# A pre-norm transformer block: the output's copy, the maxima's transposition and the number of maxima in a group are placed anew

## The chip, the cores and the metric

The kernel runs on one core of one Trainium2 chip. The metric is device time in microseconds (us) for one execution. Where a profile is quoted, the engines are PE (TensorE, matrix products), PEld (its weight loads), DVE (VectorE), ACT (ScalarE), POOL (GpSimd) and SP (SyncE, which issues all DMAs here). L75 is line 75 of the kernel; most instructions are recorded by small helpers (`mm` L75, `tr` L78, `pool` L82, `act` L89, `dve` L92, `dma` L95), so tiles' names tell more than lines do.

## What is computed

One sequence of S = 2048 rows, D = 512 columns, in float32. The reference, cut to what matters:

```python
h  = x + attention(layernorm(x), wqkv) @ wo      # 32 heads of 16 columns
h2 = h + silu(layernorm(h) @ w1) @ w2            # 1792 columns in between

scores = einsum("bhqd,bhkd->bhqk", q, k) * 16 ** -0.5
o      = einsum("bhqk,bhkd->bhqd", softmax(scores), v)
```

The softmax runs over all 2048 keys.

## The kernel before, in words

**Numbers.** A value is held as a high part and a low part. In projections and MLP a product is three matrix products (high x high, low x high, high x low) in `product` (L109). The high part is a copy by ScalarE, the low part a subtraction by `low` (L97) on VectorE or GpSimd.

**Items and groups.** The attention is cut into 32 *items*, each of four heads and 512 query rows; eight items make a block of 512 rows. An item has 16 *groups*, one for each 128 keys, so there are 512 groups; `g` counts them, and `i, c = divmod(g, 16)` are the item and the place in it. In a group there are four `scores` (L474; a product of 64 rows of the array, an exponential by ScalarE into `pt`), and the four heads' `values` (L485) of two groups earlier, which add into one PSUM bank `pv`. When the last group of an item has been added (in the group c = 1 of the next item), `finish_item` (L500) copies `pv` to `pvs` and sends it off by five DMAs; sums of the exponentials come back by DMA some groups later, are inverted by VectorE (`rc`), spread by DMA (`den`), and multiplied in by GpSimd.

**Maxima.** The exponentials need each row's maximum of scores beforehand. So each item has 64 *maxima* (`maximum`, L206): a product of 48 rows into a bank `ps_m`, and a reduction over 512 columns by VectorE into `mx`. There are 2048 of them. When an item's 64 are done, `finish_max` (L219) reduces them to `nm`, GpSimd splits these in two half-precision parts, and two steps later (`WAIT`) `place_max` (L234) transposes them on TensorE (`ps_n`), copies them to `mt` and sends them by DMA into the item's queries, where the product of `scores` then adds them in. Heads lie on the upper or the lower 64 rows of the array (*halves*); a score and a maximum on different halves can run side by side. `one_max` (L266) takes the next maximum of the item in hand, on the half that is asked for, or on the other if that half has none left.

**Where the maxima go.** They are spread over the whole program: `burst` puts some beside the projections of queries, keys and values (the first 200 us), the planner `maxima(g)` (L821) says how many come in each group of the attention, and `mlp` (L637) weaves bursts into its products. The planner takes a rate from what must be done by which item, less what the MLP blocks will take (`BESIDE`), and allows three in a group, or four beside the output projection of blocks 1 to 3. In the attention, the m-th score of a group is followed by a maximum on the other half, for as many m as there are maxima.

**Blocks.** After the items 8, 16 and 24 (`FIRSTS`) a block's output projection is done in groups c = 10 to 15 of that item (`output`, L676), and two groups into the next item the MLP of the block runs by itself (`finish_block`, `mlp`): 14 steps f, each a product of 12 matrix products with w1, `gate` (L613: SiLU, high and low part), and 12 matrix products with w2 of the step before (`second`). A dictionary such as `{4: 3, 12: 3}, {8: 4}` says: three maxima after the fourth product with w1, three after the twelfth, and four after the eighth with w2. `BESIDE_C[1]` is used for the steps in `EXTRA`, `QUIET` is the step from which there are none. The last block's MLP (`finish_last`) comes at the end.

**Queues and banks.** Each engine works in the order in which the program names its instructions, and waits in that order. PSUM in the attention: one bank for `pv`, three for maxima (`sm`), four for scores and the rest (`st`). In the projections of `wqk` that follow the first four units there are two `st` and six `sm`. `place_max` uses `sm` in the attention and `st` before it. In the MLP the bank `pv` takes the products with w1, and the first of four maxima.

Of the kernel before, what the change touches and what calls it, by code (L numbers as in the profile page):

```python
# [12 lines left out]
F16 = mybir.dt.float16  # L13
# [7 lines left out]
P = 128  # L21
# [6 lines left out]
FC = F // P  # L28
NB = S // 512
# [18 lines left out]

FIRSTS = 8, 16, 24

WAIT = 2
AHEAD = 4


BESIDE = (132, 132, 106)
OUTPUT = 9

BESIDE_A = {6: 6}, {4: 4}

BESIDE_C = ({4: 3, 12: 3}, {8: 4}), ({4: 3, 10: 3}, {4: 3, 10: 4})  # L60

EXTRA = (), (), ()

QUIET = FC, FC, FC - 2


@with_exitstack
def attention_mlp_kernel(ctx: ExitStack, tc: tile.TileContext, x, wqkv, wo, w1, w2, out):
# [19 lines left out]
    def act(fn, *a, **k):  # L88
        pin(getattr(nc.scalar, fn)(*a, **k))  # L89
# [38 lines left out]
    def bank(name, kind="st", dtype=F32):  # L128
        return banks[kind].tile([P, 512], dtype, tag=kind, name=name)
# [103 lines left out]

    def place_max(i, ns):  # L234

        ps = bank("ps_n", "sm" if at["attention"] else "st", F16)
        tr(ps[:32, :P], ns.rearrange("p j r a -> p (j r a)"), ident_h)
        mt = small.tile([32, P], F16, name="mt")
        act("copy", mt, ps[:32, :P])
        for j in range(2):  # L240
            dst = qs[i % RING][64 * j + 48:64 * j + 50].rearrange("r a n -> r (a n)")
            pin(nc.sync.dma_start(dst.rearrange("r (a b) -> r a b", b=P), mt[16 * j:16 * j + 16, :]))
        placed.add(i)
# [2 lines left out]
    todo = {(i, j): [(i, kb, qt, a, j) for kb in range(4) for a in range(2) for qt in range(4)]  # L246
            for i in range(ITEMS) for j in range(2)}
    END = 64 * ITEMS
    at = {"item": 0, "done": 0, "half": 0, "step": 0, "due": 0, "attention": False}
    agenda = {}  # L250

    def soon(steps, fn, *a):
# [8 lines left out]
    def next_item():  # L261
        while at["item"] < ITEMS and not (todo[at["item"], 0] or todo[at["item"], 1]):
            at["item"] += 1
        return at["item"]

    def one_max(half=None, ps=None):  # L266

        i = next_item()
        if i == ITEMS:
            return  # L270
        if half is None:
            half = at["half"]
            at["half"] = 1 - half
        half = half if todo[i, half] else 1 - half
        at["done"] += 1
        if maximum(*todo[i, half].pop(0), ps):
            soon(WAIT, place_max, i, finish_max(i))

    def burst(n, *more):
        for ps in more:  # L280
# [11 lines left out]
    with ExitStack() as pa:  # L292
# [114 lines left out]
        for b in range(NB):  # L407
            units = [("qk", 1), ("qk", 0)]
            vs = [("v", t) for t in range(4)]
            found = {}  # L410
            for n, (kind, k) in enumerate(vs + units if b == 0 else units + vs):
                tick()
                if b == 0 and n == 3:
                    measure()
                if kind == "v":
                    project_v(b, k)
                else:
                    project_qk(b, k)
                    if k == 0:
                        for i in range(2):  # L420
                            for h in range(4):
                                if b == 0:
                                    load_q(i, h)
                                load_k(i, h, b * 512, 512)
                if b == NB - 1:
                    burst(5)
                elif b > 0 and n > 1:
                    burst(4)
                if b + 1 < NB:
                    rows = xts[b + 1]  # L430
# [12 lines left out]
        pool("memset", va[:, :, :, DH:DH + 1], 1.0)  # L443

        pb.close()
        open_banks(pa, 1, st=2, sm=6)
        for g in range(1, NG // 2):
            for m, (b, key) in enumerate([(b, 1) for b in range(NB)] + [(b, 0) for b in range(NB)]):
# [51 lines left out]
    def finish_item(i):  # L500
# [3 lines left out]
        if i == ITEMS - 1:  # L504
            act("copy", pvs[:, :256], pv[:, :256])
            dve("tensor_copy", pvs[:, 256:], pv[:, 256:])
        else:
            act("copy", pvs, pv)
        if i == ITEMS - 1:
            last.append(pvs)  # L510
            return
# [98 lines left out]
    def turn_rows(t):  # L610
        turn(hx.pop(t), hth[:, :, t * P:(t + 1) * P], htl[:, :, t * P:(t + 1) * P])

    def gate(ps):  # L613
        g, gh, gl = (bp.tile([P, 512], dt, tag="pt", name=name)
                     for name, dt in (("g", F32), ("gh", F32R), ("gl", F32R)))
        act("activation", g, ps, AF.Silu)
        act("copy", gh, g)
        low(gl, g, gh)
        return gh, gl

    def second(b, acc, f, gh, gl, inserts={}):
# [15 lines left out]
    def mlp(b):  # L637
# [10 lines left out]
        for f in range(FC):  # L648
# [11 lines left out]
            for kind, n in (("w2", f), ("w1", f + 1)) if f else (("w1", 1), ("w2", 0)):  # L660
# [1 line left out]
            ps = pv if f else first  # L662
            weave(product(ps, lambda c: w1h[:, c, :], lambda c: w1l[:, c, :],
                          lambda c: hth[:, c, :], lambda c: htl[:, c, :], DC), beside_1)
            parts = gate(ps)
            if f == FC - 1:

                act("activation", small.tile([P, 1], F32, name="sw"), ident[:, :1], AF.Exp)
# [152 lines left out]
    def maxima(g):  # L821
# [12 lines left out]
        if g in marks or g - 1 in marks:  # L834

            return 0
        most = 4 if i in FIRSTS and OUTPUT < c < OUTPUT + 5 else 3
        n = max(0, min(most, int(at["due"]), ready - at["done"]))
        at["due"] -= n
        return n  # L840
# [3 lines left out]
    for g in range(groups):  # L844
        tick()
        i, c = divmod(g, KC)
        if g in marks:
            finish_block(i // 8 - 1, (g - 2, g - 1))
        if i + RING - 1 < ITEMS and 6 <= c < 14:
# [23 lines left out]
                    soon(5, split_weights, "w1", f, "dve", "dve")  # L873
        if g == 1:
            dve("memset", pv, 0.0)
        n = maxima(g)
        for m in range(4):
            k = m ^ (g % 2)
# [42 lines left out]
```

## Time and profile before

| | |
|---|---|
| median of 3 runs | 1712.84 us (1711.66 to 1714.91) |
| the profiled execution | 1715.59 us |
| its span, first to last instruction | 1713.8 us |
| mean granted TensorE clock | 0.998 |
| reductions `mx<-ps_m` on DVE | 2013 in 1261.5 us busy |
| exponentials `pt<-ps_s` on ACT | 2048 in 1017.8 us busy |
| copies `pvs<-pv` on ACT | 32 in 20.5 us busy |

The profile is one execution on the chip. Busy times are sums over an engine's instructions; matrix products are pipelined, so their durations overlap and a busy TensorE is not one at its peak. The *chain of waits* follows the last instruction back: at each step to what released it, or to the instruction before it on its engine. Its lines give the start, the length, the engine, the tile written and the number of instructions. A *window* is a stretch of the span with each engine's busy time in it. In groups of instructions, the numbers behind the bar are the busy time in us, the mean duration in ns, and the engine's idle time before them with what ended it.

### The profile page before, as it was taken

Reading aid. Unit: us, or ns where it says so; the run is one execution under the profiler, and the core shown is the slowest. Engines: PE = TensorE matmul, PEld = TensorE weight load, DVE = VectorE, ACT = ScalarE, POOL = GpSimd, SP = SyncE. Lnnn points to the kernel's source line nnn. Section 1 sums busy time; section 2 is a strip of 40 time slices with the busy share of each in tenths; the row PEclk is TensorE's granted clock in tenths of the full one; section 3 lists DMA queues with packets and bytes.
Section 4 is the critical chain, followed back from the end, with each engine's and each line's share of the span. In section 5 each row is a group of like instructions: output and inputs, shape, how many; then the busy total and the mean of one; then the engine's idle time right before and its main releaser. Section 6 shows DMA issues by size and latency. Waiting matters only on the chain.

```text
span 1713.8 us, 28253 instructions
## 1 busy us (share of the span) xinstructions
PE 1672.5 (98%) x10498; PEld 647.6 (38%) x10498; DVE 1449.2 (85%) x2399; ACT 1254.9 (73%) x2494; POOL 233.2 (14%) x318
## 2 busy tenths in 40 slices
PE   7999999999999999999989999999999999999999
PEld 5656422222245542222235542222235542221377
DVE  6899999999978889999978889999978869997243
ACT  4323599999963369999963369999963379999743
POOL 2113300000033310000033310000023310000000
PEclk9999999999999999999999999999999999999999
DMA  6334411111222211111222211111212211100222
GB/s 186 99 85 139 123 33 44 36 44 43 59 60 79 68 49 31 36 46 41 60 58 81 62 53 32 36 41 46 57 56 84 64 46 39 35 11 20 57 80 80
DMA packets 100570, 102.81 MB, mean 60 GB/s; under 512 B 19028, under 2 KB 77204, under 8 KB 100432
## 3 DMA queue, kind: packets, MB, share of 16 engines
q1 hardware_dynamic: 100432, 101.01, 20.2%
q8 instruction: 82, 1.34, 0.3%
q14 instruction: 56, 0.46, 0.1%
HBM read 77.72 MB, written 17.29 MB: 55 GB/s over the span
## 4 chain that ended last, share of the span: by engine, by line
PE 56%; ACT 37%; DVE 4%; issue 2%; DMA 1%; POOL 0%; SPq 0%; ACTq 0%; POOLq 0%; DVEq 0%
ACT pt L89 36%; PE pv L75 18%; PE ps_acc L75 10%; PE ps_s L75 8%; PE ps_m L75 7%; PE ps_qk L75 5%; PE ps_v L75 3%; PE ps_w L75 3%; DVE mx L215 2%; PE ps_wo L75 2%; PE ps_tr L78 1%; ACT pvs L89 1%; DVE ot L92 0%; DVE st L92 0%; DVE gl L92 0%
## 5 line engine op out<-in xcount | busy, mean ns | idle before, releaser
L215 DVE TENSOR_REDUCE mx<-ps_m 128x1 f32<-128x512 f32 x2013 | 1261.5, 684 | 104.7 <-PE ps_m L75 74.2
L89 ACT ACTIVATE pt<-ps_s 128x512 f32<-128x512 f32 x2048 | 1017.8, 662 | 16.2 <-PE ps_m L75 9.6
L75 PE MATMUL ps_s<-qs,ks 64*128 64x512 f16 x2048 | 546.2, 380 | 8.0 <-ACT pt L89 2.4
L75 PE MATMUL pv<-pt,va 128*17 128x512 f32 x4096 | 538.3, 599 | 1.3
L75 PE MATMUL ps_m<-ks,qs 48*128 48x512 f16 x2013 | 516.7, 381 | 7.7 <-DVE mx L215 6.9
L75 PEld LDWEIGHTS <-ks 64*128 64x128 f16 x2048 | 152.6, 95 | 547.0 <-issue 438.3
L75 PEld LDWEIGHTS pv<-pt,va 128*17 128x17 f32 x4096 | 68.8, 95 | 234.5 <-issue 219.5
L75 PEld LDWEIGHTS <-qs 48*128 48x128 f16 x2048 | 120.2, 94 | 69.6 <-issue 65.4
L89 ACT CAST w2h<-w 128x512 fp32r<-128x512 f32 x56 | 34.8, 621 | 90.8 <-PE ps_acc L75 90.8
L89 ACT ACTIVATE g<-pv 128x512 f32<-128x512 f32 x39 | 23.3, 598 | 103.8 <-PE pv L75 103.8
L82 POOL TENSOR_SCALAR nm<-nm 128x16 f32<-128x16 f32 x32 | 8.5, 265 | 663.3 <-DVE nm L222 663.3
L75 PE MATMUL ps_acc<-w2l,gh 128*128 128x512 f32 x224 | 92.6, 413 | 0.0
L75 PE MATMUL ps_acc<-w2h,gh 128*128 128x512 f32 x224 | 92.2, 412 | 0.0
L75 PE MATMUL ps_acc<-w2h,gl 128*128 128x512 f32 x224 | 88.2, 394 | 0.0
L92 DVE TENSOR_TENSOR gl<-g,gh 128x512 fp32r<-128x512 f32 x56 | 41.2, 736 | 53.3 <-ACT gh L89 53.3
L82 POOL TENSOR_TENSOR w2l<-w,w2h 128x512 fp32r<-128x512 f32 x42 | 53.5, 1274 | 182.3 <-ACT w2h L89 182.3
L75 PE MATMUL pv<-hth,w1l 128*128 128x512 f32 x156 | 65.5, 420 | 0.0
L82 POOL TENSOR_TENSOR ot<-ot,den 128x512 f32<-128x512 f32 (+1 forms) x16 | 20.4, 1274 | 317.6 <-DMA den<-dr 286.6
L89 ACT ACTIVATE ks<-ps_qk,qk_s 128x512 f32<-128x512 f32 x24 | 16.6, 690 | 62.5 <-PE ps_qk L75 62.5
L75 PE MATMUL pv<-hth,w1h 128*128 128x512 f32 x156 | 62.1, 398 | 0.0
L75 PE MATMUL pv<-htl,w1h 128*128 128x512 f32 x156 | 61.4, 394 | 0.0
L82 POOL TENSOR_TENSOR w1l<-w,w1h 128x512 fp32r<-128x512 f32 x42 | 55.6, 1324 | 15.5 <-ACT w1h L89 15.5
(119 smaller groups left out, 1315.9 us busy)
## 6 DMA issues: line engine op xcount, KB each, us to landing
w<-in_B_w_dram SPq DMA_DIRECT2D x112, 256.0 KB
ks<-kd SPq DMA_DIRECT2D x120, 192.0 KB
qs<-qd SPq DMA_DIRECT2D x128, 48.0 KB
kd<-sh SPq DMA_DIRECT2D x16, 256.0 KB
qd<-sh SPq DMA_DIRECT2D x16, 256.0 KB
hx<-in_A_x_dram SPq DMA_DIRECT2D x16, 256.0 KB
out_dram<-ot SPq DMA_DIRECT2D x16, 256.0 KB
ot<-pvs SPq DMA_DIRECT2D x124, 32.0 KB
```

Source lines behind the costliest of these rows:

```text
L75: tc.keep_in_program_order(nc.tensor.matmul(*a, **k))
L78: tc.keep_in_program_order(nc.tensor.transpose(*a))
L82: tc.keep_in_program_order(getattr(nc.gpsimd, op)(*a, **k))
L89: pin(getattr(nc.scalar, fn)(*a, **k))
L92: pin(getattr(nc.vector, fn)(*a, **k))
L215: pin(nc.vector.tensor_reduce(mx[i][:, j, a, qt, kb:kb + 1], ps, axis=AX.X, op=ALU.max))
```

## The change

- `finish_item`: `pv` is copied by VectorE, except for the items 8, 16, 24 (ScalarE as before) and the last one.
- `place_max`: always takes a bank `sm`; in the attention VectorE copies to `mt`.
- `due_at` (new): a transposition that falls due in the attention is put off to the next group with c = 2 (`JOINT`), which follows the group that ends with the output's copy, unless that is too near the item's own scores or in an item after 8, 16 or 24. In a group c = 2 the planner allows two maxima.
- `one_max`: where the half asked for has none left, it takes the next item's, if that item's operands are loaded and the item in hand is more than 12 groups away; in the first projections it takes from items 0 and 1, whichever has the earlier keys.
- Planner: at most three maxima in all other groups, also beside the output projection.
- MLP: steps 4, 7 and 10 of the first two blocks have 13 maxima; the first burst comes after the fifth product; the last block has maxima up to step 12; `gate` of the first step subtracts on GpSimd.
- First projections: six maxima beside the last block's queries and keys (five before); from the second block on, the scaled product goes to SBUF and its low part `sl` is made by GpSimd.

```diff
+JOINT = 2
-BESIDE = (132, 132, 106)
+BESIDE = (141, 141, 122)
+BESIDE_V = (0, 4), (0, 4), (6, 5)
-BESIDE_C = ({4: 3, 12: 3}, {8: 4}), ({4: 3, 10: 3}, {4: 3, 10: 4})
+BESIDE_C = ({5: 3, 12: 3}, {8: 4}), ({4: 3, 10: 3}, {4: 3, 10: 4})
-EXTRA = (), (), ()
+EXTRA = (4, 7, 10), (4, 7, 10), ()
-QUIET = FC, FC, FC - 2
+QUIET = FC, FC, FC - 1
...
     def place_max(i, ns):
-        ps = bank("ps_n", "sm" if at["attention"] else "st", F16)
+        ps = bank("ps_n", "sm", F16)
...
-        act("copy", mt, ps[:32, :P])
+        if at["attention"]:
+            dve("tensor_copy", mt, ps[:32, :P])
+        else:
+            act("copy", mt, ps[:32, :P])
...
+    def due_at(i):
+        g = at["group"]
+        if g is None:
+            return WAIT
+        joint = g + WAIT + (JOINT - g - WAIT) % KC
+        return joint - g if joint < KC * i - 2 and joint // KC - 1 not in (-1, *FIRSTS) else WAIT
...
     def one_max(half=None, ps=None):
...
+        if at["blocks"]:
+            i = min(range(2), key=lambda n: (todo[n, half] or todo[n, 1 - half] or [(n, KC)])[0][1])
+        elif not todo[i, half] and 64 * (i + 2) <= at["ready"] and KC * i - at["next"] > 12:
+            i += 1
...
-            soon(WAIT, place_max, i, finish_max(i))
+            soon(due_at(i), place_max, i, finish_max(i))
...
-                    project_qk(b, k)
+                    project_qk(b, k, scale=b > 0)
...
-                if b == NB - 1:
-                    burst(5)
-                elif b > 0 and n > 1:
-                    burst(4)
+                if b:
+                    burst(BESIDE_V[b - 1][kind == "v"])
...
     def finish_item(i):
...
-        else:
-            act("copy", pvs, pv)
+        elif i in FIRSTS:
+            act("copy", pvs, pv)
+        else:
+            dve("tensor_copy", pvs, pv)
...
-    def gate(ps):
+    def gate(ps, engine="dve"):
...
-        low(gl, g, gh)
+        low(gl, g, gh, engine)
...
-            parts = gate(ps)
+            parts = gate(ps, "dve" if f else "pool")
...
     def maxima(g):
...
-        most = 4 if i in FIRSTS and OUTPUT < c < OUTPUT + 5 else 3
+        at["ready"] = ready
+        most = 2 if c == JOINT and i and i - 1 not in FIRSTS else 3
```

More of the change, by code (lines that the diff above doesn't have):

```diff
@@ L248, in attention_mlp_kernel @@
     END = 64 * ITEMS
-    at = {"item": 0, "done": 0, "half": 0, "step": 0, "due": 0, "attention": False}
+    at = {"item": 0, "done": 0, "half": 0, "step": 0, "due": 0, "attention": False, "group": None, "ready": 0, "next": 0, "blocks": True}
     agenda = {}
@@ L445, in attention_mlp_kernel @@
         pb.close()
+        at["blocks"] = False
         open_banks(pa, 1, st=2, sm=6)
@@ L846, in attention_mlp_kernel @@
         i, c = divmod(g, KC)
+        at["group"], at["next"] = None, g
         if g in marks:
@@ L875, in attention_mlp_kernel @@
             dve("memset", pv, 0.0)
+        at["group"] = g
         n = maxima(g)
```

## The prediction

> **What bounds the kernel now.** I read the page's busy shares and chain first, then the chain of waits inside the attention, then windows of the other stages.
>
> ```profile
> PE 1672.5 (98%) x10498; PEld 647.6 (38%) x10498; DVE 1449.2 (85%) x2399; ACT 1254.9 (73%) x2494; POOL 233.2 (14%) x318
> PE 56%; ACT 37%; DVE 4%; issue 2%; DMA 1%; POOL 0%; SPq 0%; ACTq 0%; POOLq 0%; DVEq 0%
> ```
>
> TensorE hardly rests, and the chain changes between it and ScalarE. Now the chain in one item of the attention, in which `ps_s` are scores, `ps_m` maxima and `pv` the value products:
>
> ```profile
> 302.84 0.48 ACT pvs L89
> ...
> 305.72 0.98 PE pv L75 x8
> 306.70 0.32 PE ps_s L75
> 307.02 0.22 PE ps_m L75 x2
> ...
> 307.68 0.98 PE pv L75 x8
> ...
> 335.46 29.45 ACT pt L89 x60
> ```
>
> A group lasts 1.96 us (305.72 to 307.68): 0.98 of values and 0.98 of four score slots, in which the three maxima run beside scores on the other half of the array's rows. ScalarE's four exponentials come to the same: 29.45 / 60 x 4 = 1.96. So 16 groups are 31.4 us, and two things come on top in each item. The first is the output's copy, read from TensorE's timeline:
>
> ```profile
> 301.30 1.05 PE L75 MATMUL pv<-pt,va 128*17 128x512 f32 x8
> ...
> 303.37 1.05 PE L75 MATMUL pv<-pt,va 128*17 128x512 f32 x8
> ...
> 305.65 0.62 PE L75 MATMUL pv<-pt,va 128*17 128x512 f32 x4
> ```
>
> Two groups take 4.35 us where 3.92 is usual: 0.43 lost. Only 0.11 of it is the value product's own wait for the copy (2.07 between the first two); the rest comes a group later, because ScalarE is 0.48 behind and score banks come free late. The second is the maxima's transposition, `ps_n`, here from the chain:
>
> ```profile
> 277.61 0.98 PE pv L75 x8
> 278.59 0.04 PE ps_n L78
> ...
> 279.81 0.98 PE pv L75 x8
> ```
>
> 2.20 instead of 1.96: 0.24 lost. ScalarE copies `ps_n` between exponentials, and `ps_n` takes one of three banks that the maxima use.
>
> **The change, part by part.** Counts of groups come from following the planner's arithmetic in `maxima` and, for the new kernel, `due_at`.
>
> *The output's copy to VectorE.* 28 of 31 copies move (items 8, 16, 24 stay).
>
> ```profile
> L92 DVE COPY pvs<-pv x1: 424/424/424, 1615.1 to 1615.1; 128x256 f32<-128x256 f32 x1
> 546.25 1.88 DVE L215 TENSOR_REDUCE mx<-ps_m 128x1 f32<-128x512 f32 x3
> 301.99 0.68 DVE L215 TENSOR_REDUCE mx<-ps_m 128x1 f32<-128x512 f32 x1
> 335.50:367.40 31.90, 31.79 (x240) 7.04 (x240) 29.59 (x50) 31.90 (x67) 1.96 (x4) 1.00 0.17 41
> ```
>
> (The last row is a window of an item: its ends, its length, then each engine's busy time, PE, PEld, DVE, ACT, POOL, with instructions.) No copy of 512 columns from PSUM by VectorE is in the trace. Half of one takes 0.42 us, and twice that is an upper end, 0.85; a reduction over 512 such columns is 0.68, the lower. I take 0.69, near the reduction. Reductions follow each other every 0.60 us ((1.88 - 0.68) / 2). Behind the copy on VectorE stand the next group's reductions, and TensorE's maxima wait for these; TensorE's next value product waits for the copy itself. The group's third reduction starts at 301.99, so the copy would start at about 302.6 and end at 303.3, where ScalarE's ended at 303.32: TensorE loses 0.06 to 0.11, as now. ScalarE is not delayed any more, so the other 0.32 goes. VectorE in the next group then has 0.69 + 2 x 0.60 = 1.89 us instead of 1.80: this is why that group has two maxima, and it ends just inside 1.96. Sum: 28 x (0.43 - 0.08) = -9.8 us; from -12.0 (all goes) to 0 (VectorE's lag costs as much as ScalarE's).
>
> [...]
>
> *Transpositions.* Before, 24 fall in attention groups, each at some 0.27 (0.24 above, up to 0.31 elsewhere). After, 12 wait for the group of the copy, where a bank and time are spare; I charge 0.1 (the small reduction `nm` ahead of it still falls in some group of three). 11 stay alone, with `mt` copied by VectorE in a group of three maxima:
>
> ```profile
> L89 ACT COPY mt<-ps_n 32x128 f16<-32x128 f16 x32 | 8.1, 255 | 14.5 <-PE ps_n L78 14.5
> ```
>
> Its cost on VectorE lies between nothing and the 0.42 of the copy of 256 columns above; this one has 128, and it delays reductions; I charge 0.25, ScalarE's own. Sum: 1.2 + 2.8 - 6.5 = -2.5 us; from -5 to +3.
>
> *Halves.* Maxima that have no partner on the other half take a score slot of 0.22. Before there is none in the attention; two-maxima groups and the new order upset the balance, and `i += 1` mends all but 13 of them. 13 x 0.22 = +2.8 us (0 to +5).
>
> *Beside the MLP.* 30 maxima leave the attention: 28 go to the MLP blocks (two blocks 132 to 141, the last 116 to 126), two to the projections. In the attention they were free on TensorE; here not. Windows of a step with ten maxima and one with none:
>
> ```profile
> 546.78:554.72 7.94, 7.94 (x36) 4.61 (x35) 6.95 (x13) 2.36 (x4) 2.52 (x2) 1.00 0.51 151
> 1376.80:1382.33 5.53, 5.53 (x25) 4.50 (x24) 2.04 (x4) 2.37 (x4) 2.53 (x2) 1.00 0.00 0
> 547.79 0.76 PE L75 MATMUL ps_m<-ks,qs 48*128 48x512 f16 x3
> 548.48 0.50 PE L75 MATMUL pv<-hth,w1l 128*128 128x512 f32 x1
> ...
> 550.55 0.60 PE L75 MATMUL ps_m<-ks,qs 48*128 48x512 f16 x3
> 551.08 0.50 PE L75 MATMUL ps_acc<-w2h,gh 128*128 128x512 f32 x1
> ```
>
> Ten cost 2.41 us in three bursts, 0.80 each. A step of the last block gets ten: +2.4. Six steps go from three bursts to four with 13 maxima: at least 0.8 each, and VectorE, busy 6.95, would need 6.95 + 3 x 0.60 = 8.75, and stands still while `gl` waits behind ScalarE, so up to 1.8; I take 1.3: +7.8. The first burst moves from the fourth matmul to the fifth: now it takes 0.69 (547.79 to 548.48) against the second's 0.53, as VectorE is still at the four maxima before it; 28 steps x 0.16 = -4.5. And `gl` of each block's first step leaves VectorE for GpSimd:
>
> ```profile
> 515.34 1.62 DVE L92 TENSOR_TENSOR gl<-g,gh 128x512 fp32r<-128x512 f32 x1
> 518.80 0.37 PE L75 MATMUL ps_m<-ks,qs 48*128 48x512 f16 x1 [0.23 <-DVE mx L215]
> ```
>
> The bursts about it wait for VectorE; I take 0.8 for each block, -2.4 (0 to -3.6). GpSimd has time for it, since the value is needed one product later. Sum: +3.3 us (-3 to +8).
>
> [...]
>
> *Three maxima beside the output projection.* Item 8 has three now, items 16 and 24 four:
>
> ```profile
> 477.59:504.97 27.38, 25.78 (x150) 12.72 (x150) 19.68 (x37) 16.37 (x33) 10.13 (x13) 1.00 0.27 78
> 863.00:892.83 29.83, 25.84 (x149) 12.82 (x146) 20.97 (x39) 16.22 (x32) 10.07 (x13) 1.00 0.26 75
> 1249.60:1279.49 29.89, 26.79 (x154) 12.98 (x154) 22.03 (x41) 16.26 (x33) 10.11 (x14) 1.00 0.22 65
> ```
>
> The same groups, 2.45 and 2.51 longer: -5.0 us (-2 to -5).
>
> *Projections.* `ps_n` takes a maxima's bank there instead of a projection's. A unit with it against one without:
>
> ```profile
> 110.69:115.48 4.79, 4.17 (x21) 2.40 (x20) 3.56 (x7) 1.47 (x3) 1.46 (x2) 1.00 0.66 131
> 115.48:119.19 3.71, 3.71 (x21) 2.39 (x19) 3.69 (x7) 1.31 (x2) 0.55 (x1) 1.00 0.63 136
> ```
>
> Three times 1.08; 0.4 may stay, as VectorE is full (3.69 of 3.71): -2.0 (0 to -3.2). The second half `sl` on GpSimd, and bursts of six in the last block, I put at nothing: ScalarE is busy 1.3 of 3.7 there, and a burst's sixth maximum fills a slot that five leave half empty. If GpSimd were late for the layer norm's `rs`, it would cost up to 1 us in each of two blocks.
>
> *Reciprocals.* Where the eighth item of a block ends, `rc` is due early:
>
> ```profile
> DVE rc L92 <- DMA rc<-dn: 15.1, 2, 14.8
> ```
>
> 0.3 us of waiting now; as the groups before it shrink by 0.35, VectorE will wait in three items, and maxima behind it: +0.8.
>
> Total: -9.8 - 2.5 + 2.8 + 3.3 - 5.0 - 2.0 + 0.8 = **-12.4 us**. The profiled execution took 1715.59 us, its span 1713.8; it becomes 1703.2. The median of the runs is 2.75 lower, 1712.84, so I forecast **1700.4 us**.
>
> **Rivals.** (1) *VectorE becomes the bound in the copy's group: slower.* If the missing maximum brings nothing, because with three banks the next maxima stand behind the copy whatever their number, TensorE pays the copy's full 0.69 in 28 groups, and the transposition beside it 0.25 in 12. Then the copies give 28 x (0.69 - 0.43) = +7.3 and the transpositions nothing: -12.4 + 9.8 + 2.5 + 7.3 = +7.2, **1720.0 us**. The kernel is slower than before once a copy's group loses over 0.52 us (0.08 + 12.4 / 28). For it: VectorE was busy 29.59 of 31.90 in an item. Against: the reckoning above, 1.89 in 1.96.
> (2) *Half gain.* The copy's group loses 0.25, and 13 maxima cost 1.8 a step: +4.8 + 3.0, so -4.6, **1708.2 us**. For it: 31.90 - 29.59 leaves VectorE 0.14 us a group, and any lag over that goes through the banks to TensorE.
> (3) *Grouping fails.* Transpositions do not meet their copies, or unpaired maxima cost two slots: +1.8 + 2.9, so -7.7, **1705.1 us**. Half the transpositions stay alone by the planner's own rule.
>
> **Numbers.** Forecast 0.60 (1692 to 1705), rival 3 0.10, rival 2 0.20, rival 1 0.10. About 0.2% (3.4 us) is what a measurement of this kernel can tell from no change, so faster means under 1709.4. Rival 2 lies on that edge and is shared between faster and same: faster 0.80, same 0.10, slower 0.10. The range, 1691 to 1712, takes in rivals 2 and 3 and the better ends of the copies and the MLP steps; it leaves out rival 1 and some tails.
>
> **What would show it.** Right: items of 31.5 to 31.8 us in the attention, value products 2.0 apart over the copy, `mx` waiting little; MLP steps of 9.2 with 13 maxima, 7.8 with ten; 27.4 in all three output windows. Wrong: `ps_m` waiting for `mx` after each copy (rival 1), steps above 9.7, or `pv` more than 2.2 apart at each copy.

## The result and the profile after

| | before | changed |
|---|---|---|
| median of 5 runs each | 1713.0 us (1711.66 to 1715.86) | 1705.64 us (1704.41 to 1706.8) |
| ratio, 95% interval | | 0.9952 [0.9937, 0.9966] |
| span of the profiled execution | 1713.8 us | 1703.9 us |
| the changed kernel measured again (below) | 1714.85 us | 1704.41 us, 0.994 [0.9926, 0.9953] |

The change makes the kernel faster by about half a per cent: 7.4 and 10.4 us by the two medians, 9.9 us by the two profiled spans. The forecast was 12.4 us off the profile, or 1700.4 us. In the changed kernel the helpers' lines move by four: `mm` L79, `tr` L82, `act` L93, `dve` L96; maxima's reduction is L219, the small reduction `nm` L226.

From the page of the changed kernel, busy times and the chain's shares:

```profile
PE 1668.5 (98%) x10498; PEld 645.3 (38%) x10498; DVE 1458.5 (86%) x2447; ACT 1242.2 (73%) x2443; POOL 241.0 (14%) x327
PE 87%; ACT 7%; DVE 4%; DMA 1%; issue 1%; SPq 0%; POOL 0%; ACTq 0%; POOLq 0%; DVEq 0%
```

Busy shares hardly move; the chain does. ScalarE's share of it falls from 37% to 7%. Its four exponentials take about as long as TensorE's group, 1.96 us: the group right behind a copy on ScalarE still lasted 1.92, so ScalarE could make up only 0.04 of its delay there. Without the copies it keeps up, and TensorE leads, though ScalarE stays busy in all of an item (31.42 of 31.42 us in the first window below).

**The output's copy.** From the timeline of the changed kernel, VectorE and then TensorE's value products at the start of an item (start, length, engine, line, operation, tiles, count, and in brackets an idle time and who ended it):

```profile
333.24 0.68 DVE L96 COPY pvs<-pv 128x512 f32<-128x512 f32 x1
333.84 0.20 DVE L96 COPY mt<-ps_n 32x128 f16<-32x128 f16 x1
333.97 1.27 DVE L219 TENSOR_REDUCE mx<-ps_m 128x1 f32<-128x512 f32 x2
...
329.99 1.05 PE L79 MATMUL pv<-pt,va 128*17 128x512 f32 x8
...
331.95 1.05 PE L79 MATMUL pv<-pt,va 128*17 128x512 f32 x8
...
333.97 1.05 PE L79 MATMUL pv<-pt,va 128*17 128x512 f32 x8
...
335.93 1.05 PE L79 MATMUL pv<-pt,va 128*17 128x512 f32 x8
```

The value product that waits for the copy comes 2.02 after the one before (331.95 to 333.97) and the next 1.96 later: the two groups over the copy lose 0.06 where 0.43 was lost. The transposition's copy `mt` falls into the same group, and VectorE is still through with that group's two maxima in time. Windows of the changed kernel (ends, length, busy time of PE, PEld, DVE, ACT, POOL with instructions, granted clock, DMA share, GB/s): an item, the three output windows, a unit of the second projections with a transposition in it, and the steps f = 4 to 7 of the first MLP block, with 13, 10, 10 and 13 maxima:

```profile
329.44:360.86 31.42, 31.41 (x242) 7.04 (x240) 30.27 (x50) 31.42 (x65) 1.28 (x1) 1.00 0.17 43
474.70:501.97 27.27, 25.76 (x150) 12.80 (x150) 19.67 (x37) 16.25 (x33) 10.08 (x13) 1.00 0.28 81
859.87:887.11 27.24, 25.62 (x149) 12.58 (x142) 19.33 (x36) 16.20 (x33) 10.10 (x13) 1.00 0.27 81
1244.31:1271.59 27.28, 25.77 (x150) 12.79 (x150) 19.68 (x37) 16.25 (x33) 10.10 (x13) 1.00 0.28 81
131.19:135.28 4.09, 4.09 (x20) 2.40 (x19) 3.55 (x7) 1.46 (x3) 1.29 (x2) 1.00 0.38 112
535.01:544.34 9.33, 9.11 (x38) 4.72 (x37) 8.52 (x15) 2.36 (x4) 2.52 (x2) 1.00 0.00 0
544.34:552.16 7.82, 7.82 (x35) 4.61 (x34) 7.14 (x13) 2.36 (x4) 2.52 (x2) 1.00 0.50 152
552.16:559.90 7.74, 7.74 (x35) 4.60 (x34) 6.86 (x12) 2.36 (x4) 2.53 (x2) 1.00 0.26 69
559.90:569.63 9.73, 9.35 (x39) 4.63 (x37) 9.11 (x17) 2.80 (x5) 3.16 (x5) 1.00 0.00 0
```

Items 4, 12, 20 and 27, called plain items below, have neither a transposition outside the copy's group nor an unpaired maximum. They take 31.42 us, 0.06 over 16 x 1.96; before, they took 31.81. The output windows of items 16 and 24 fall from 29.83 and 29.89 to 27.24 and 27.28, item 8's length. The unit with a transposition falls from 4.79 to 4.09. MLP steps with ten maxima fall from 7.94 to 7.74; those with 13 take 9.3 to 9.7. The step f = 7 was already longer in the kernel before, as a transposition lies at its end; its window there:

```profile
562.65:571.17 8.52, 8.23 (x37) 4.51 (x35) 7.33 (x14) 2.36 (x4) 3.17 (x5) 1.00 0.00 0
```

**Where the forecast's terms went.** All lengths below are distances between starts of instructions in the two traces: first exponentials of groups in the attention, first w1 products of steps in the MLP.

| term | forecast | measured | from |
|---|---|---|---|
| output's copy | -9.8 | -10.9 | 28 x (31.42 - 31.81) |
| transpositions | -2.5 | -0.6 | the 24 items away from output and MLP take 6.0 more than 24 plain ones, before and after; so -1.2 if the halves cost +1.2; +0.28 each in items 9 and 17 |
| halves | +2.8 | +1.2 | an estimate: six groups or so of 2.17 in place of 1.96, others nearly free |
| reciprocals | +0.8 | +1.4 | group c = 6 of items 16 and 24: 1.96 to 2.86, 2.28 to 2.74 |
| beside the MLP | +3.3 | +5.5 | blocks 101.30 to 103.67, 100.96 to 103.68, 98.38 to 98.82 |
| output projection | -5.0 | -5.2 | windows above |
| projections | -2.0 | -0.1 | first exponential at 199.03 and at 198.92; counted from the first transposition, -0.9 |
| not in the sum | | -1.2 | the group before the output windows, 3.54 to 2.78 in item 16, and small change |
| total | -12.4 | -9.9 | |

Four terms missed by 1.6 us or more: the transpositions and the halves, which nearly cancel, the MLP and the projections. Only the sum of the transpositions and halves is measured, about +0.5 where +0.3 was forecast; how it divides is an estimate. Two rows owe much to the execution that was profiled: the group c = 6 of item 16 takes 2.06 to 2.86 us, and the group before its output window 2.4 to 3.7, in kernels that don't differ there.

### The profile page after: what moved, and what is told of

It reads as the page before. It is cut to its first block, busy times and chain, and to the rows that moved or that the text cites. A ratio compares the mean times of both kernels' runs of the same rounds, so it can differ in the third digit from the quotient of the medians.

```text
span 1703.9 us, 28237 instructions
## 1 busy us (share of the span) xinstructions
PE 1668.5 (98%) x10498; PEld 645.3 (38%) x10498; DVE 1458.5 (86%) x2447; ACT 1242.2 (73%) x2443; POOL 241.0 (14%) x327
## 4 chain that ended last, share of the span: by engine, by line
PE 87%; ACT 7%; DVE 4%; DMA 1%; issue 1%; SPq 0%; POOL 0%; ACTq 0%; POOLq 0%; DVEq 0%
PE pv L79 33%; PE ps_s L79 19%; PE ps_m L79 11%; PE ps_acc L79 9%; ACT pt L93 6%; PE ps_qk L79 5%; PE ps_w L79 3%; PE ps_wo L79 3%; PE ps_v L79 3%; DVE mx L219 2%; PE ps_tr L82 1%; DVE pvs L96 0%; SPq L99 0%; DMA va<-in_A_wqkv_dram 0%; ACT gh L93 0%
## 5 line engine op out<-in xcount | busy, mean ns | idle before, releaser
L219 DVE TENSOR_REDUCE mx<-ps_m 128x1 f32<-128x512 f32 x2012 | 1260.7, 683 | 89.2 <-PE ps_m L79 62.1
L93 ACT ACTIVATE pt<-ps_s 128x512 f32<-128x512 f32 x2048 | 1012.9, 610 | 22.2 <-PE ps_m L79 17.0
L79 PE MATMUL ps_s<-qs,ks 64*128 64x512 f16 x2048 | 538.3, 380 | 4.5 <-ACT pt L93 1.5
L79 PE MATMUL pv<-pt,va 128*17 128x512 f32 x4096 | 538.3, 599 | 1.6 <-DVE pvs L96 0.4
L79 PE MATMUL ps_m<-ks,qs 48*128 48x512 f16 x2012 | 514.1, 381 | 4.9 <-DVE mx L219 4.3
L79 PEld LDWEIGHTS <-ks 64*128 64x128 f16 x2048 | 150.3, 95 | 549.4 <-issue 440.3
L79 PEld LDWEIGHTS pv<-pt,va 128*17 128x17 f32 x4096 | 68.7, 95 | 229.1 <-issue 210.9
L79 PEld LDWEIGHTS <-qs 48*128 48x128 f16 x2048 | 119.3, 94 | 66.9 <-issue 60.7
L93 ACT CAST w2h<-w 128x512 fp32r<-128x512 f32 x56 | 34.7, 620 | 106.1 <-PE ps_acc L79 106.1
L93 ACT ACTIVATE g<-pv 128x512 f32<-128x512 f32 x39 | 23.3, 597 | 108.5 <-PE pv L79 108.5
L79 PE MATMUL ps_acc<-w2l,gh 128*128 128x512 f32 x224 | 92.1, 411 | 0.0
L79 PE MATMUL ps_acc<-w2h,gh 128*128 128x512 f32 x224 | 91.3, 407 | 0.0
L79 PE MATMUL ps_acc<-w2h,gl 128*128 128x512 f32 x224 | 89.3, 399 | 0.0
L96 DVE TENSOR_TENSOR gl<-g,gh 128x512 fp32r<-128x512 f32 x53 | 36.3, 685 | 50.2 <-ACT gh L93 50.2
L93 ACT ACTIVATE ks<-ps_qk,qk_s 128x512 f32<-128x512 f32 x30 | 20.7, 689 | 74.1 <-PE ps_qk L79 71.2
L79 PE MATMUL pv<-htl,w1h 128*128 128x512 f32 x156 | 64.8, 416 | 0.0
L79 PE MATMUL pv<-hth,w1l 128*128 128x512 f32 x156 | 62.6, 402 | 0.0
L79 PE MATMUL pv<-hth,w1h 128*128 128x512 f32 x156 | 62.5, 401 | 0.0
```

Source lines behind the costliest of these rows:

```text
L79: tc.keep_in_program_order(nc.tensor.matmul(*a, **k))
L96: pin(getattr(nc.vector, fn)(*a, **k))
L219: pin(nc.vector.tensor_reduce(mx[i][:, j, a, qt, kb:kb + 1], ps, axis=AX.X, op=ALU.max))
```

## The experiments

Short diffs are against the changed kernel, if nothing else is said. Each run's `before` is the kernel before on the same chip.

**One part alone: the copy.** Against the kernel before:

```diff
-        else:
+        elif i in FIRSTS:
             act("copy", pvs, pv)
+        else:
+            dve("tensor_copy", pvs, pv)
```

> The kernel before with one edit: the output's copy on VectorE, with three maxima in the group behind it. Theory (the copy pays only because the group behind it has room): VectorE then has 0.69 + 3 x 0.60 = 2.49 us of work in a group of 1.96, the overrun of some 0.5 goes through the three banks to TensorE, so a copy costs 0.4 to 0.5 as it did on ScalarE, and the time stays within 1710 to 1716. Rival (it is the relief of ScalarE alone that pays): the copy's group costs 0.1, 28 x 0.35 = 9.8 us less, 1703. Value products over a copy: 4.3 to 4.5 us for two groups by the theory, 4.0 by the rival.

Measured: 1712.72 us (1711.15 to 1714.01) beside 1713.69, ratio 0.9993 [0.9984, 1.0002]. No gain, as expected. But the place of the loss was missed, and it is the more instructive part: the two groups over the copy take 3.98 us, as the rival had it, and not 4.3 to 4.5. The timeline of this kernel, VectorE and then TensorE:

```profile
333.84 0.68 DVE L92 COPY pvs<-pv 128x512 f32<-128x512 f32 x1
334.44 3.67 DVE L215 TENSOR_REDUCE mx<-ps_m 128x1 f32<-128x512 f32 x6
...
335.56 0.60 PE L75 MATMUL ps_m<-ks,qs 48*128 48x512 f16 x2
...
336.37 0.37 PE L75 MATMUL ps_m<-ks,qs 48*128 48x512 f16 x1
...
336.89 1.05 PE L75 MATMUL pv<-pt,va 128*17 128x512 f32 x8
```

The value product waits no longer over the copy than in the changed kernel (groups of 1.96 and 2.02). But VectorE has 0.60 more to do and only 1.96 - 1.80 = 0.16 of room in a group. It runs six reductions without a pause, and the third maximum of the *next* group has no bank before the third of these reductions ends: 334.44 + 2 x 0.60 + 0.68 = 336.32, and the maximum starts at 336.37, 0.81 after the group's first pair (335.56), where an undisturbed group has 0.45. That group lasts 2.31. So the loss is 0.06 + 0.35 = 0.41 a copy, against 0.43 before: nearly the same loss, moved from ScalarE's banks to VectorE's. Plain items take 31.68 to 31.78 us.

**One part undone: the copy back on ScalarE.**

```diff
-            dve("tensor_copy", pvs, pv)
+            act("copy", pvs, pv)
```

> The changed kernel with one edit: the output's copy back on ScalarE, all else as changed (two maxima in the copy's group, the transposition beside it on VectorE). Theory (most of the gain is this copy): 0.39 us in each of 28 items comes back, +11, 1716 to 1717, slower than the kernel before by some 0.2%. Rival (fewer maxima in the group and the grouping bring the gain by themselves): the group with two maxima has a score slot to spare and lets ScalarE catch up, so under +4, below 1710.

Measured: 1715.08 us (1712.58 to 1717.89) beside 1713.69, ratio 1.0005 [0.9996, 1.0014]; 9.4 above the changed kernel's median. The same item as above, by the windows of this kernel:

```profile
331.88:363.64 31.76, 31.63 (x242) 7.04 (x240) 29.77 (x49) 31.76 (x67) 1.28 (x1) 1.00 0.18 42
```

ScalarE is busy in all of the 31.76 and runs 67 instructions there instead of 65. The groups over the copy are 2.39 and 1.92 again; each plain item is 0.34 longer. As expected: without this one line nothing is left of the net gain.

**One part undone: three maxima in the copy's group.**

```diff
-        most = 2 if c == JOINT and i and i - 1 not in FIRSTS else 3
+        most = 3
```

> The changed kernel with one edit: up to three maxima in the copy's group too (the planner's total is the same, and the two-maxima groups come elsewhere). Theory (VectorE's room decides): 2.49 us, or 2.7 with the transposition's copy, of VectorE in a group of 1.96: a copy's group costs 0.4 to 0.6 instead of 0.06, 25 x 0.4 = +10, 1714 to 1718. Rival (VectorE's lag is absorbed by the groups behind): +0 to +3, 1705 to 1708.

Measured: 1713.46 us (1712.48 to 1717.1) beside 1713.69, ratio 1.0 [0.9991, 1.0009]. The window of item 4 in this kernel:

```profile
330.78:362.75 31.97, 31.84 (x242) 7.03 (x240) 30.29 (x50) 31.41 (x66) 1.27 (x1) 1.00 0.17 42
```

0.55 longer than in the changed kernel. ScalarE needs 31.41 of it, so it isn't ScalarE that holds this item up. The copy's stretch has a group of 2.31 where the copy stands alone and one of 2.62 or 2.63 where the transposition comes with it. In items 6, 7 and 22 the planner happens to give two maxima to the group right behind, and there nothing is lost: 2.02 and then 1.92. So the room may also come one group later. With the last two runs this settles the main point, by plain items: 31.81 us before, 31.68 to 31.78 with the copy on VectorE and three maxima, 31.76 with two maxima and the copy on ScalarE, 31.42 with both.

**One part undone: transpositions placed when they fall due.**

```diff
-            soon(due_at(i), place_max, i, finish_max(i))
+            soon(WAIT, place_max, i, finish_max(i))
```

> The changed kernel with one edit: transpositions two steps after their last maximum, as before, and not put off to the copy's group; two maxima there as changed. Theory (a transposition in a group of three maxima costs about 0.25, beside the copy next to nothing): eleven come to stand alone, +2 to +3, 1707.5 to 1709. Rival (a transposition beside the copy costs as much, or alone as little, since VectorE copies it in either place): within 1 us of the changed kernel.

Measured: 1705.24 us (1705.02 to 1706.79) beside 1713.69, ratio 0.9953 [0.9939, 0.9966]: as the changed kernel. An item whose transposition is taken out of the copy's group is 0.00 to 0.13 longer, 0.75 us over all of them. The reason is in item 3. First the changed kernel's timeline, VectorE:

```profile
320.76 0.22 DVE L226 TENSOR_REDUCE nm<-mx 128x16 f32<-128x64 f32 x1
320.89 2.47 DVE L219 TENSOR_REDUCE mx<-ps_m 128x1 f32<-128x512 f32 x4
```

and that of this experiment, VectorE and TensorE:

```profile
318.96 0.22 DVE L226 TENSOR_REDUCE nm<-mx 128x16 f32<-128x64 f32 x1
...
321.22 0.22 PE L82 MATMUL ps_n<-ident_h,ns 128*32 128x128 f16 x1
```

In the changed kernel no transposition follows `nm` here, as it was put off to the next copy; the group still lasts 2.27. In the experiment it follows at once, and the group lasts 2.31. So it is the small reduction, in a group of three maxima, that costs most of the time, and the change doesn't move it.

**The same question from the other side: `mt` copied by ScalarE everywhere.**

```diff
-        if at["attention"]:
-            dve("tensor_copy", mt, ps[:32, :P])
-        else:
-            act("copy", mt, ps[:32, :P])
+        act("copy", mt, ps[:32, :P])
```

> The changed kernel with one edit: ScalarE copies mt in the attention again, transpositions stay where the change puts them. Theory (since the grouping turned out to bring under 1 us, the engine of this small copy does not matter much beside the copy either: ScalarE has room once the output's copy is gone): items whose transposition falls beside the copy stay within 0.1 us of 31.42 to 31.74, those with one alone within 0.1 of 31.7 to 32.2, the time within 1.5 us of the changed kernel. Rival (the copy on ScalarE was what a transposition cost): 0.2 to 0.3 us more in 23 items, +5 to +7.

Measured in a single execution: 1704.09 us. The 24 items away from output and MLP agree with the changed kernel's within 0.03 us, but for item 15 (31.64 instead of 31.94, and 31.67 in two other kernels that don't differ there); where `mt` stands beside the copy the groups are 2.07 and 1.92 instead of 2.00 and 1.98, nearly the same sum. Items 9 and 17 are 33.36 instead of 33.64. So the engine that copies `mt` is worth nothing, and 0.28 the wrong way in two items.

**One part undone: the next item's maxima.**

```diff
-        elif not todo[i, half] and 64 * (i + 2) <= at["ready"] and KC * i - at["next"] > 12:
+        elif False:
```

> The changed kernel with one edit: where a half has none left, the other half of the same item is taken, as before (the next item's maxima are not). Theory: the planner's arithmetic gives 14 maxima without a partner either way, only in other groups, so the attention is the same within 1 us; each group with one or two of them lasts 2.1 to 2.2 us instead of 1.96. Rival (the forecast's picture, in which the next item's maxima mend the halves): 10 to 20 more score slots of 0.22, +2 to +4 us.

Measured in a single execution: 1703.16 us; the attention without output and MLP stages takes 972.7 us, against 974.4 and 974.2 in the two profiles of the changed kernel, so the rule brings no gain there. Following the planner again, there are 14 maxima without a partner with the rule or without it: it moves them, it doesn't remove them. So the prediction's sentence that the rule mends all but 13 was wrong in its reason, though not in the count. And not each of them costs a slot: groups of 2.17 stand beside others of 2.00.

**The changed kernel once more.** No edit.

> The changed kernel unaltered, on the same chip as the others, to see what an execution varies by. Theory: 1704 to 1707 as before; between profiles only the start (first transposition at 8.0 to 9.3 us in the profiles so far) and the output projection of item 16, which waits for DMAs, differ. Rival (it varies all over the attention): items differ by over 0.1 us from one profile to the other.

Measured: 1704.41 us (1703.12 to 1705.52) beside 1714.85, ratio 0.994 [0.9926, 0.9953]. The 24 items away from output and MLP agree with the first profile within 0.04 us; the MLP blocks within 0.07. What differs is the start (first transposition at 8.23 instead of 9.33) and item 24's group c = 6 (2.36 instead of 2.74).

**MLP steps with 13 maxima: GpSimd makes their `gl`.**

```diff
-            parts = gate(ps, "dve" if f else "pool")
+            parts = gate(ps, "dve" if f and f not in EXTRA[b] else "pool")
```

> The changed kernel with one edit: in the MLP steps with 13 maxima the low part gl is made by GpSimd, as it is in step 0. Theory (such a step is long because VectorE stands still at gl, which waits for ScalarE, while banks wait for VectorE): the four-maxima burst takes 0.55 to 0.7 us instead of 1.15 to 1.23, a step 8.5 to 8.8 instead of 9.3, six steps -3 to -5 us: 1701 to 1703. [...]

First what it is to mend: the changed kernel's timeline in the first step with 13 maxima, VectorE and then TensorE:

```profile
540.93 0.69 DVE L96 TENSOR_TENSOR gl<-g,gh 128x512 fp32r<-128x512 f32 x1 [0.33 <-ACT gh L93]
541.54 1.88 DVE L219 TENSOR_REDUCE mx<-ps_m 128x1 f32<-128x512 f32 x3
...
543.48 0.37 PE L79 MATMUL ps_m<-ks,qs 48*128 48x512 f16 x1 [0.23 <-DVE mx L219]
```

`gl` waits for ScalarE, the three reductions behind it wait for `gl`, and TensorE's last burst for these. Measured: 1701.98 us (1701.55 to 1703.3) beside 1712.67, ratio 0.9939 [0.9926, 0.9953]. The same step and the next by the windows of this kernel:

```profile
534.34:543.03 8.69, 8.69 (x38) 4.45 (x36) 7.74 (x14) 2.40 (x5) 3.81 (x3) 1.00 0.00 0
543.03:551.09 8.06, 8.02 (x35) 4.71 (x35) 7.30 (x13) 2.31 (x4) 2.52 (x2) 1.00 0.49 147
```

9.33 falls to 8.69, but the step after rises from 7.82 to 8.06. Both blocks get 1.0 us shorter, 2.0 in all, less than the 3 to 5 expected. The stall was there, but a good third of the gain (0.24 of 0.64) is given back: VectorE's load moves into the next step. The interval overlaps both of the changed kernel's, so by its time alone this version is not told apart from it; by the steps it is.

**Three mends at once:** the edit above, bursts of five instead of six in the first projections, and one of the output's reciprocals a group later.

```diff
-BESIDE_V = (0, 4), (0, 4), (6, 5)
+BESIDE_V = (0, 4), (0, 4), (5, 5)
...
-        steps = (1, 4, 5, 7) if u == 7 else (2, 6, 8, 10)
+        steps = (1, 5, 5, 7) if u == 7 else (2, 6, 8, 10)
...
-            parts = gate(ps, "dve" if f else "pool")
+            parts = gate(ps, "dve" if f and f not in EXTRA[b] else "pool")
```

> The changed kernel with three edits: gl on GpSimd in the steps with 13 maxima; five maxima instead of six beside the last block's queries and keys; the reciprocal of a block's last item one group later. Theory: -3 to -5 for gl; -1.5 for the bursts (two bursts of 1.5 us become 0.75, because there are five maxima banks in that stage); 0 to -1.7 for the reciprocal, if the spread that follows is not late for the output projection: in all -5 to -8, 1698 to 1701. Rival (each only shifts its wait): within 2 us of the changed kernel.

The bursts of six, in the changed kernel's timeline of TensorE, with the two waits ahead of a layer norm's transpositions:

```profile
43.24 0.63 PE L82 MATMUL ps_tr<-ident,ks 128*128 128x128 f32 x4 [1.41 <-issue]
...
65.84 0.63 PE L82 MATMUL ps_tr<-ident,ks 128*128 128x128 f32 x4 [1.41 <-ACT ks L93]
...
84.23 0.82 PE L79 MATMUL ps_m<-ks,qs 48*128 48x512 f16 x5
85.40 0.37 PE L79 MATMUL ps_m<-ks,qs 48*128 48x512 f16 x1 [0.35 <-DVE mx L219]
85.71 0.50 PE L79 MATMUL ps_qk<-xth,wqk_h 128*128 128x512 f32 x1
```

and the same places in the kernel before:

```profile
42.62 0.63 PE L78 MATMUL ps_tr<-ident,ks 128*128 128x128 f32 x4 [1.24 <-issue]
...
65.04 0.63 PE L78 MATMUL ps_tr<-ident,ks 128*128 128x128 f32 x4 [1.23 <-ACT sh L89]
...
83.41 0.82 PE L75 MATMUL ps_m<-ks,qs 48*128 48x512 f16 x5
84.16 0.50 PE L75 MATMUL ps_qk<-xth,wqk_h 128*128 128x512 f32 x1
...
87.10 0.70 PE L75 MATMUL ps_m<-ks,qs 48*128 48x512 f16 x4
88.03 0.37 PE L75 MATMUL ps_m<-ks,qs 48*128 48x512 f16 x1 [0.23 <-DVE mx L215]
88.33 0.50 PE L75 MATMUL ps_v<-wv_h,xth 128*128 128x512 f32 x1
```

A burst of six takes 1.48 (84.23 to 85.71), one of five 0.75 (83.41 to 84.16). In this part of the program `sm` has five banks (`open_banks(pb, 0, st=3, sm=5)`), so the sixth maximum waits until VectorE has read the first. The second burst of six takes 1.48 as well (88.67 to 90.15), but the burst of five at its place took 1.23 in the kernel before (87.10 to 88.33): VectorE was late for it, as its own `sl` of 0.75 us stood ahead of the reductions, and the change moves `sl` to GpSimd. With six banks, six maxima take no longer than five do here: 0.75 in the second projections of a run below (156.50 to 157.25).

Measured: 1701.77 us (1699.77 to 1704.01) beside 1712.67, ratio 0.9933 [0.9919, 0.9947]: no better than the edit to `gl` alone. Both mends did what they were for: in this kernel no TensorE wait is left in that stretch, and VectorE's wait for the reciprocal is gone. But fewer maxima early means that item 8's are done one group later, and its scores need them:

```profile
455.94 0.39 PE L79 MATMUL ps_s<-qs,ks 64*128 64x512 f16 x1 [1.54 <-DMA qs<-mt]
```

This line of TensorE's timeline in this kernel shows the first score of item 8 waiting for the DMA that carries its maxima. Item 7's last group is 3.57 instead of 1.96, and the group before the output windows of items 8 and 24 is 2.66 instead of 2.43.

**Two mends, and the total of early maxima moved to another burst.**

```diff
-BESIDE_V = (0, 4), (0, 4), (6, 5)
+BESIDE_V = (0, 4), (0, 5), (5, 5)
...
-            parts = gate(ps, "dve" if f else "pool")
+            parts = gate(ps, "dve" if f and f not in EXTRA[b] else "pool")
```

> The changed kernel with gl on GpSimd in the steps with 13 maxima, and bursts of five instead of six beside the last projection block's queries and keys; the maxima that these leave out go beside the block before (five instead of four at each of its four value units). Theory: -2.0 for gl (as the traces showed), -1.5 for the two bursts (five maxima banks in that stage), +0.8 for four bursts that need a third score slot, and no item's transposition comes later than before: -2.5 to -3, 1702.5 to 1703.5 if the changed kernel is 1705.6. Rival (only a shift of waits): within 1 us of the changed kernel.

Measured: 1705.67 us (1705.19 to 1708.31) beside 1714.85, ratio 0.9949 [0.9936, 0.9963]; 1702.5 to 1703.5 was expected, and it is 1.3 above the changed kernel on the same chip (1704.41). The bursts are short and the MLP blocks 0.9 shorter, as they should be, but in the second projections there is a new gap. TensorE's weight loads, then its products, and two windows of this kernel (the third number from the right is the granted clock):

```profile
151.20 0.25 PEld L79 LDWEIGHTS <-qs 48*128 48x128 f16 x2 [2.94 <-DMA qs<-qd]
...
148.14 0.61 PE L79 MATMUL ps_m<-ks,qs 48*128 48x512 f16 x4
151.23 0.74 PE L79 MATMUL ps_m<-ks,qs 48*128 48x512 f16 x2 [2.48 <-DVE mx L219]
...
152.49 0.63 PE L79 MATMUL ps_qk<-xth,wqk_l 128*128 128x512 f32 x1
152.92 0.63 PE L79 MATMUL ps_qk<-xtl,wqk_h 128*128 128x512 f32 x1
...
151.23:155.00 3.77, 3.77 (x10) 2.16 (x10) 1.29 (x2) 0.14 (x1) 1.16 (x1) 0.55 0.45 161
156.00:160.00 4.00, 4.00 (x21) 2.52 (x19) 3.07 (x6) 1.37 (x4) 1.15 (x1) 1.00 0.43 156
```

The products' line names a reduction as releaser, but VectorE had been done; the weight load's line names the true one, the DMA that brings the next item's queries. With one maximum more beside each value projection the loaded items are used up sooner, and the next one's queries have not landed. Then the clock falls as well (last section).

**Four maxima beside the output projection, none extra in the first MLP block.**

```diff
-BESIDE = (141, 141, 122)
+BESIDE = (132, 141, 122)
-EXTRA = (4, 7, 10), (4, 7, 10), ()
+EXTRA = (), (4, 7, 10), ()
...
-        most = 2 if c == JOINT and i and i - 1 not in FIRSTS else 3
+        most = 2 if c == JOINT and i and i - 1 not in FIRSTS else 4 if i in FIRSTS and OUTPUT < c < OUTPUT + 5 else 3
```

> The changed kernel with one trade undone: four maxima beside the output projection again (in 11 of 12 groups by the planner's arithmetic, item 8's too), and in return no step with 13 maxima in the first block. Theory: the output projection of items 8, 16, 24 is longer by 1.9, 2.45, 2.5 (VectorE is the bound there with four), the first block's MLP shorter by 3 x 1.4 = 4.2: +2.7, 1708. Rival (the longer output projections of the kernel before had another cause than the fourth maximum, a DMA or the queue's position): those stages stay as they are, -4.2, 1701.

Measured: 1706.36 us (1705.05 to 1709.14) beside 1712.67, ratio 0.9966 [0.9953, 0.9978]. The three output windows of this kernel:

```profile
472.85:501.91 29.06, 26.46 (x153) 12.89 (x153) 21.46 (x40) 16.24 (x32) 10.07 (x13) 1.00 0.27 75
855.07:884.94 29.87, 26.78 (x154) 12.98 (x154) 22.04 (x41) 16.24 (x32) 10.07 (x13) 1.00 0.25 74
1243.34:1273.23 29.89, 26.80 (x154) 12.98 (x154) 22.06 (x41) 16.25 (x32) 10.08 (x13) 1.00 0.26 73
```

They are 1.79, 2.63 and 2.61 longer than in the changed kernel, with 3, 4 and 4 maxima more by TensorE's counts (the second window of the changed kernel lacks a record): 0.60 to 0.66 for each. The first MLP block is 5.0 shorter with nine fewer (114.86 to 109.82 with its surroundings): 0.56 for each. As expected, the two places are priced almost alike, so moving a maximum from the one to the other gains little. Not foreseen: the last groups of items 15 and 23 take 3.46 and 3.31 in place of 1.96, as the next item's first scores wait for the DMA of their maxima, the wait of the run with three mends.

## Why the prediction was right, and where it was not

**The copy** (forecast -9.8, measured -10.9) was right in each step. The copy takes 0.68 on VectorE, where 0.69 was taken. On ScalarE the copy took 0.65 in the kernel before (median), so it became no shorter; what pays is the queue in which it stands. Two maxima make room and three don't: the run with three loses 0.41 or more at a copy, unless the next group has two, and comes out level with the kernel before. The extra 1.1 is that a plain item gains 0.39 and not the 0.35 reckoned. Rival 1 (slower, if a copy loses over 0.52) was held off by a smaller margin than the chance of 0.10 suggests: with three maxima a copy alone loses 0.41, beside a transposition 0.7. Its mechanism is the one that shows when the group of two is missing.

**The transpositions** (-2.5, measured -0.6) failed in size. The step charged 0.25 to 0.27 for a lone transposition and 0.1 for a grouped one. The two runs show that grouping is worth 0.75 us in all and the engine of `mt` nothing, but for items 9 and 17. What a lone one seemed to cost is mostly the reduction `nm` that comes with it: 0.07 to 0.31 in items 2, 3, 10, 11, 18 and 19 of the changed kernel, where no transposition follows it. Why it differs so much from place to place was not tried. The prediction named `nm` in brackets and didn't price it. This is the effect that rival 3 named, but not by its way: transpositions do meet their copies (as `mt` at 333.84 does), only it brings little.

**Halves** (+2.8, measured +1.2): the count held by accident and its reason fell, as above.

**Reciprocals** (+0.8, measured +1.4): right in kind, but in two items (16 and 24) and not three, and its size varies between executions as said above. The wait in item 16, in a line of VectorE's timeline of the changed kernel:

```profile
851.17 0.25 DVE L96 RECIPROCAL rc<-rc 128x16 f32<-128x16 f32 x1 [0.89 <-DMA rc<-dn]
```

**Beside the MLP** (+3.3, measured +5.5). The steps with 13 maxima were right: 1.4, 1.2 and 1.4 more, 8.0 for six against 7.8 forecast. So was the last block's step, +2.2 against +2.4. What was mis-sized are the two gains set against it. The stall of the first burst goes (7.94 to 7.74), but steps behind a long one keep part of it (7.82) and others had none to lose: -3.2 in place of -4.5. And the first steps' `gl` on GpSimd gives 9.42 to 8.73, 9.09 to 8.47 and 9.10 to 8.70, less 0.22 in the step ahead in one block: -1.5 in place of -2.4, since VectorE still has its maxima to reduce there. How much of a burst's 0.80 is the wait for VectorE, and what makes up the rest, no run here separates. One of the signs named for "wrong" was touched: the steps f = 7 take 9.73 and 9.74, over 9.7; they were the longer ones before, too.

**Output projection** (-5.0, measured -5.2): right, and the run with four brings the cost back in all three windows.

**Projections** (-2.0, measured -0.1, or -0.9 from the first transposition) is the step that failed. Its first half held: three units lose 0.70 each (the first two 4.79 to 4.09), -2.1. Its second half did not: bursts of six "I put at nothing", because a sixth maximum fills half a slot. That looked at TensorE's slots and not at the banks; the row used for it came from the second projections, where `sm` has six. Against the kernel before, the two bursts cost 0.73 and 0.25, +1.0; against bursts of five behind an idle VectorE, 0.73 each. The low part `sl` on GpSimd stands ahead of the layer norm's `rs` and costs 0.17 and 0.18 more (waits of 1.24 and 1.23 become 1.41 each), not the "up to 1 us" that was named. That leaves -0.8, and from the first transposition to the first exponential 0.9 is gained in both profiles of the changed kernel (190.50 to 189.59 and 189.58). Over all profiles that differ in nothing there this stretch varies by more, 189.2 to 190.9, so the agreement is partly luck. In the first profile the start is 0.8 later (first transposition at 9.33 against 8.53), which varies from run to run.

Of the other rivals, the half gain (1708.2 us) didn't come: a copy's groups lose 0.06 and not 0.25. Rival 3's time, 1705.1, lies next to the median measured, but that is mostly chance: of its two halves only the lost gain of the transpositions is there, and most of what the sum lacks is in the projections and the MLP, less a better copy. The first median, 1705.64, lies just above the forecast's own band (1692 to 1705) and inside the range; the second, 1704.41, lies inside both. So the mechanism of the main term is shown, and the size of the whole is off by a sixth to two fifths of the forecast gain.

## What to carry to other kernels

Moving work to another in-order engine paid here only where that engine's own queue was made shorter at the same place or right behind; move it and make the room in one change, and look for the loss not at the moved instruction but where the banks that lie between run out, a group or two later. Before making a burst longer, count the banks of the pool that is open at that place: six maxima take 0.75 us with six banks and 1.48 with five. Where a schedule is tight against its operands' DMAs on one side and their deadline on the other, taking single pieces out of an early burst or adding them there can bring a wait of 1.5 to 2.5 us for a saving of 0.7, as in two runs here.

## What the runs showed of the hardware

- In the run with the gap of 2.48 us, TensorE comes back slower: the granted clock is 0.50 from 151.37 to 154.78 (0.55 in the window shown), products of 512 columns last 0.63 and follow each other every 0.43 (152.49 to 152.92), where 0.39 and 0.23 are usual. Six products take 2.85 us there up to the transposition (151.90 to 154.75), where the changed kernel's unit has 1.59 (131.19 to 132.78): 1.3 us lost on top of the gap. Full pace is back from 154.91 on (products of 0.39 every 0.23 from 155.25; the clock is 1.00 in the second window shown). After gaps of 1.41 and 1.54 us, above, the next products are at full pace (0.39 each).
- The clock was lower also without such a gap ahead of it: in all 13 profiles it is 0.50 for 6.8 us at the start of the attention, before and after the change alike, though TensorE has no gap of over 0.7 us in the 40 us ahead of it (the longest is 0.62 in the kernel before and 0.29 in the changed one). A window of the changed kernel:

```profile
201.43:208.26 6.83, 6.63 (x25) 1.01 (x24) 5.54 (x10) 4.32 (x9) 1.03 (x2) 0.50 0.82 203
```

  In six of the 13 profiles (the runs with the copy alone, the copy back, three maxima, transpositions when due, three mends and two mends) it is 0.50 for 3.4 us in the output projection of item 16 as well, where a group then takes 6.6 in place of 5.1. Neither the kernel before nor the changed one has this in its profile.
- The start of the program varies: the first transposition starts between 7.57 and 9.33 us over 13 profiles. In the two profiles of the changed kernel it accounts for 1.1 of the 1.3 us between their spans (1703.9 and 1702.6).
- The group before the output window of item 16 takes 2.44 to 3.68 us in kernels that don't differ there. Why it varies in this item alone was not tried and stays open.
